# Talking-heads attention and two feed-forward layers on one core: the first chunk's loads, spreads and score copies in another order

## The chip, the core and the metric

One core of a Trainium2 chip runs the whole program. The metric is the device time of one execution in microseconds, the median of several runs; lower is better. TensorE (PE) multiplies, VectorE (DVE), ScalarE (ACT) and GpSimd (POOL) do elementwise work, each with a queue that is worked through in order. SyncE (SP) only issues DMAs; ScalarE can issue them too. The moves themselves are done by 16 DMA engines.

## The reference

```python
B, H, S, D = 2, 12, 448, 64          # q, k, v: (B, H, S, D), float32
scores = (q @ k^T) / sqrt(D)
scores = einsum('bhij,hg->bgij', scores, w_pre)     # mixes the 12 heads
attn   = softmax(scores, axis=-1)
attn   = einsum('bhij,hg->bgij', attn, w_post)      # mixes them again
x = (attn @ v) as (896, 768)
h = x @ w_in;  x = (h * clip(h + 3, 0, 6) / 6) @ w_out            # 768 -> 2048 -> 768
h = x @ w2_in; x = P(h) / (Q(h) + 1e-6) @ w2_out                  # P, Q: polynomials in h, |h|
```

Products are made to float32 precision from two parts: a high half (rounded) and a low half (the rest), and three matrix products of them.

## The kernel before

**Tiling.** A *chunk* is 120 query rows of one batch (88 in a batch's last one, nine groups), eight chunks in all; the code counts them from `C = 0`, the text calls them chunk one, two, three. A *group* is ten query rows of all 12 heads, 120 partitions; a chunk has 12 groups (`G`). `m` counts groups through all chunks.

**Scores.** `scores(C, hp)` makes two heads' scores of a chunk, 120 query rows by 448 keys each, into two PSUM banks `sc` (six products, line 267). Two copies (line 270) bring them to SBUF: one by ScalarE, one by VectorE.

**Spreads.** The mixing of heads wants the 12 heads of a query row in 12 partitions, so the scores are moved by DMA into `full`, 120 partitions by 12 groups by 448. For chunk one the copies go to one large tile `stage`, and `spread_group` moves one group at a time, 12 DMAs (line 252). From chunk two on, each head's copy `stg` is moved by `spread` as soon as it is made, 12 DMAs again (line 249), and a group can only be used when all 12 have landed. All are issued by SP.

**A step** of the loop over groups: `gsplit(m + 2)` makes the high half `sh` and low half `sl` of the group after next (lines 286 and 288, GpSimd; two buffers each), `premix(m)` mixes the heads (three products, lines 298 to 300, "mixing m"), takes the maximum (VectorE, line 302) and the exponential (ScalarE, line 304), `norm` and `weigh` put the sum's reciprocal into `wr`, `postmix(m - 2)` mixes again (line 333, "postmix"), and its result is copied to `at` (ScalarE, line 337) in the next step.

**Order.** It is written out by hand. In the loop over chunks, `SST` says in which steps the next chunk's score pairs are made, `QST` in which steps `q_prep` splits the q of the chunk after next (ScalarE the high half, VectorE the low), `AVST` in which the products with v are made (from chunk two on, for the chunk before). What a step makes is copied in the next one: the first pair's first half ahead of the split, its second half behind it, the second pair behind the maximum. Chunk one's scores and the first two pairs of chunk two come ahead of the loop. DMAs are issued in program order on SP; `load_q(C + 2)` and, in step 1 of chunk one, four `load_v` and `load_ab` (the small vectors pa, pb) are written in the loop but wait for nothing, and stand on SP ahead of the spreads, which wait for the copies. `build_ab` works on pa and pb in the first step of chunk two.

After the eight chunks the two feed-forward layers follow, from about 235 us on, in which TensorE works on 128x512 products.

Of the kernel before, what the change touches and what calls it, by code (L numbers as in the profile page):

```python
# [26 lines left out]
NP = H // 2  # L27
# [21 lines left out]
def fused_kernel(  # L49
# [201 lines left out]
    def spread_group(C, g, st):  # L251
        nc.sync.dma_start(out=full[C][:, g, :], in_=st.rearrange("(i g) h s -> g i (h s)", g=chunks[C][3])[g])

    def scores(C, hp, tags=("sc", "sc"), st=None, second=nc.vector.tensor_copy):
# [19 lines left out]
        post(2, lambda: take(0, nc.scalar.copy), lambda: take(1, second))  # L274
# [3 lines left out]
    def gsplit(m, eng=nc.gpsimd):  # L278
        if m >= len(groups):
            return  # L280
        C, g = groups[m]
        r = GP
        sh = att.tile([GP, S], F32R, tag="sh", bufs=2, name=f"sh{m}")
        sl = att.tile([GP, S], F32R, tag="sl", bufs=2, name=f"sl{m}")
        s = full[C][:, g, :]
        eng.tensor_scalar(out=sh[:r], in0=s[:r], scalar1=1.0, scalar2=0.0, op0=ALU.mult, op1=ALU.add)  # L286
        ssp[m] = (sh, sl)
        return eng.tensor_tensor(out=sl[:r], in0=s[:r], in1=sh[:r].bitcast(F32), op=ALU.subtract)  # L288
# [33 lines left out]
    def postmix(m):  # L322
# [9 lines left out]
        for jc in range(JC):  # L332
# [3 lines left out]
        aposts.append(  # L336
            lambda: nc.scalar.activation(out=at[C][:, :, :, c0 : c0 + rr], in_=av, func=AF.Copy)
        )
# [139 lines left out]
    for hp in range(NP):  # L478
# [3 lines left out]
        if hp == 1:  # L482
# [3 lines left out]
               nc.scalar.copy if hp == NP - 2 else nc.vector.tensor_copy)  # L486
        flush()
    for g in range(chunks[0][3]):
        spread_group(0, g, stage)
# [6 lines left out]
    first = gsplit(0, nc.vector)  # L496
    gsplit(1)
# [7 lines left out]
    flush()  # L505

# [41 lines left out]
    LAG = 2  # L548

# [10 lines left out]
    for C, (b, r0, n, G) in enumerate(chunks):  # L560
# [7 lines left out]
        sst = SST[G] if C else SST[G][: NP - FIRST]  # L568
        if nxt is not None:
            add([lambda h=h: scores(nxt, h) for h in range(0 if C else FIRST, NP)], sst)  # L570
        if C + 2 < len(chunks):
            add([lambda: q_prep(C + 2, 0, NP // 2), lambda: q_prep(C + 2, NP // 2, NP)], QST[G])
# [8 lines left out]
        for s in range(G):  # L581
            if s == 0 and C + 2 < len(chunks):
                load_q(C + 2)
            if C == 0 and s == 1:
                for i in range(4):
                    load_v(0, i)
                load_ab()
            if C == 1 and s == 0:
# [9 lines left out]
            for p in posts[:1]:  # L598
                p[1]()
            premix(m)  # L600
            if m >= 1 and not full_step:
# [360 lines left out]
```

## Time and profile before

| | |
|---|---|
| median of 3 runs | 714.84 us (712.84 to 715.27) |
| the profiled execution, its own time | 714.0 us |
| its span, first to last instruction | 712.3 us |
| TensorE busy | 695.3 us, 98% |
| VectorE busy | 555.4 us, 78% |
| ScalarE busy | 413.5 us, 58% |
| GpSimd busy | 261.1 us, 37% |
| mean granted clock of TensorE | 0.995 |

The times of the trace are microseconds from the first instruction of the profiled execution. A wait is read from the brackets at the end of a timeline row: how long the engine was idle before the row, and what ended it. Windows of the trace give the busy time of each engine, the granted clock of TensorE (1.00 is 2.4 GHz, 0.50 is 1.2 GHz), the mean busy share of the 16 DMA engines and the rate that they moved.

### The profile page before, as it was taken

To read this page: it belongs to the slowest core of one execution; us is meant where nothing else is said; L and a number is where in the kernel's file an instruction comes from. 1 tells how busy PE (TensorE), PEld (TensorE's weight loads), DVE (VectorE), ACT (ScalarE), POOL (GpSimd) and SP (SyncE) were. 2 spreads that over 40 slices of the span, in tenths; PEclk is the share of its full clock that TensorE was granted. 3 is DMA by queue.
4 is the path that set the end of the run, shared out by engine and by line. 5 is a ranking of instruction groups with operands and counts; after the bars stand their busy time and mean duration, and the time that the engine had idled before them with its cause. 6 is when DMAs were issued, how large, how long until landed. Compare 5 with 4: busy or idle time off the path is not lost.

```text
span 712.3 us, 12369 instructions
## 1 busy us (share of the span) xinstructions
PE 695.3 (98%) x4457; PEld 618.8 (87%) x4457; DVE 555.4 (78%) x925; ACT 413.5 (58%) x855; POOL 261.1 (37%) x259
## 2 busy tenths in 40 slices
PE   6999999999999999999999999999999999999997
PEld 3778888888889888889888888879999999889997
DVE  5565585665667689889997777888988899799991
ACT  5687887787887344334332221247666766579851
POOL 3887775877777333332444454400000000000000
PEclk9899999999999999999999999999999999999999
DMA  7625476555394544454354555364755766845522
GB/s 247 227 79 160 142 211 184 165 147 159 121 254 119 154 141 143 139 160 152 120 183 154 171 185 168 96 232 133 244 189 210 243 209 225 309 167 200 183 85 89
DMA packets 76033, 122.81 MB, mean 172 GB/s; under 512 B 6804, under 2 KB 56260, under 8 KB 75972
## 3 DMA queue, kind: packets, MB, share of 16 engines
q1 hardware_dynamic: 75684, 121.66, 53.8%
q8 instruction: 35, 0.57, 0.3%
q10 hardware_dynamic: 288, 0.37, 0.2%
q14 instruction: 26, 0.21, 0.1%
HBM read 83.39 MB, written 19.27 MB: 144 GB/s over the span
## 4 chain that ended last, share of the span: by engine, by line
PE 46%; DVE 31%; DMA 10%; ACT 6%; issue 5%; POOL 1%; SPq 0%; ACTq 0%; POOLq 0%; DVEq 0%
PE A L333 9%; DVE wf L425 7%; DVE wf L421 7%; PE X L353 5%; PE acc L379 4%; PE acc L378 4%; PE acc L377 4%; DMA pre<-wf 4%; PE sc L267 4%; DMA wraw<-in_moe_w_in_dram 4%; DVE gl L542 4%; DVE wf L419 4%; PE M L298 3%; PE h L378 3%; PE h L379 3%
## 5 line engine op out<-in xcount | busy, mean ns | idle before, releaser
L379 PE MATMUL h<-xh,wl 128*128 128x512 f32 (+1 forms) x384 | 141.0, 367 | 1.6 <-DVE wl L445 1.6
L377 PE MATMUL h<-xh,wh 128*128 128x512 f32 (+1 forms) x384 | 141.7, 369 | 0.0
L378 PE MATMUL h<-xl,wh 128*128 128x512 f32 (+1 forms) x384 | 140.7, 366 | 0.6 <-DVE xl L742 0.6
L417 ACT ACTIVATE wf<-wraw 128x768 f32<-128x768 f32 (+1 forms) x56 | 48.7, 877 | 98.4 <-DMA pre<-wf 55.9
L288 POOL TENSOR_TENSOR sl<-full,sh 120x448 fp32r<-120x448 f32 x89 | 102.4, 1150 | 7.4
L302 DVE TENSOR_REDUCE st<-M 120x1 f32<-120x448 f32 x90 | 56.1, 623 | 56.0 <-PE M L300 55.8
L333 PEld LDWEIGHTS A<-wr,e 120*112 120x112 f32 x720 | 86.5, 177 | 8.9 <-ACT wr L317 4.5
L333 PE MATMUL A<-wr,e 120*112 120x120 f32 x720 | 89.2, 267 | 2.0 <-ACT wr L317 1.9
L441 POOL TENSOR_SCALAR wh<-wf 128x768 fp32r<-128x768 f32 (+1 forms) x34 | 32.7, 962 | 138.5 <-DVE wf L425 135.8
L304 ACT ACTIVATE e<-M,st 120x448 f32<-120x448 f32 x90 | 57.2, 636 | 44.7 <-DVE st L302 44.6
L379 PEld LDWEIGHTS h<-xh,wl 128*128 128x128 f32 x384 | 72.1, 188 | 11.5 <-DVE wl L445 2.6
L378 PEld LDWEIGHTS h<-xl,wh 128*128 128x128 f32 x384 | 72.1, 188 | 8.9 <-DVE xl L742 0.9
L377 PEld LDWEIGHTS h<-xh,wh 128*128 128x128 f32 x384 | 72.1, 188 | 8.4 <-ACT wh L444 0.3
L286 POOL TENSOR_SCALAR sh<-full 120x448 fp32r<-120x448 f32 x89 | 55.3, 621 | 45.5 <-PE M L299 36.5
L379 PE MATMUL y<-gh,wl 128*128 128x384 f32 x192 | 70.2, 366 | 0.6 <-POOL wl L442 0.6
L377 PE MATMUL y<-gh,wh 128*128 128x384 f32 x192 | 70.4, 367 | 0.0
L378 PE MATMUL y<-gl,wh 128*128 128x384 f32 x192 | 70.2, 366 | 0.0
L442 POOL TENSOR_TENSOR wl<-wf,wh 128x768 fp32r<-128x768 f32 (+1 forms) x34 | 67.7, 1991 | 2.8
L421 DVE SCALAR_TENSOR_TENSOR wf<-wraw,icst,wf 128x768 int32<-128x768 int32 (+1 forms) x56 | 61.9, 1105 | 1.0
L419 DVE TENSOR_SCALAR wf<-wf 128x768 int32<-128x768 int32 x66 | 42.5, 643 | 24.0 <-ACT wf L417 23.8
L425 DVE SCALAR_TENSOR_TENSOR wf<-wraw,icst,wf 128x768 int32<-128x768 int32 (+1 forms) x56 | 57.7, 1032 | 0.6
L541 ACT ACTIVATE gh<-g 128x384 fp32r<-128x384 f32 (+1 forms) x32 | 18.6, 580 | 60.2 <-DVE g L539 59.9
(107 smaller groups left out, 1523.6 us busy)
## 6 DMA issues: line engine op xcount, KB each, us to landing
wraw<-in_moe_w_out_dram SPq DMA_DIRECT2D x28, 768.0 KB
wraw<-in_moe_w_in_dram SPq DMA_DIRECT2D x22, 768.0 KB
full<-stg SPq DMA_DIRECT2D x60, 210.0 KB
vraw<-in_v_dram SPq DMA_DIRECT2D x42, 224.0 KB
wpre<-in_moe_w_in_dram SPq DMA_DIRECT2D x10, 768.0 KB
w2h<-wh SPq DMA_DIRECT2D x16, 384.0 KB
w2l<-wl SPq DMA_DIRECT2D x16, 384.0 KB
wsh<-w2h SPq DMA_DIRECT2D x16, 384.0 KB
```

The costliest lines, as they stand in the source:

```text
L286: eng.tensor_scalar(out=sh[:r], in0=s[:r], scalar1=1.0, scalar2=0.0, op0=ALU.mult, op1=ALU.add)
L288: return eng.tensor_tensor(out=sl[:r], in0=s[:r], in1=sh[:r].bitcast(F32), op=ALU.subtract)
L302: nc.vector.tensor_reduce(out=st[:r, 0:1], in_=mt[:r, :S], op=ALU.max, axis=AX.X, negate=True)
L304: nc.scalar.activation(out=e[:r], in_=mt[:r, :S], func=AF.Exp, bias=st[:r, 0:1], accum_out=st[:r, 1:2])
L333: nc.tensor.matmul(av[:, jc], lhsT=e[:r, jc * JP : (jc + 1) * JP], rhs=wr[:r, :, :rr], start=True, stop=True)
L377: nc.tensor.matmul(o, lhsT=wh, rhs=mh, start=first, stop=False)
L378: nc.tensor.matmul(o, lhsT=wh, rhs=ml, start=False, stop=False)
L379: nc.tensor.matmul(o, lhsT=wl, rhs=mh, start=False, stop=last)
L419: nc.vector.tensor_scalar(out=wi, in0=wi, scalar1=3, scalar2=None, op0=ALU.logical_shift_left)
L421: nc.vector.scalar_tensor_tensor(out=wi, in0=hw, scalar=icst[:, 0:1], in1=wi, op0=ALU.bitwise_and, op1=ALU.bitwise_or)
L425: nc.vector.scalar_tensor_tensor(out=wi, in0=lw, scalar=icst[:, 1:2], in1=wi, op0=ALU.logical_shift_right, op1=ALU.bitwise_or)
L442: nc.gpsimd.tensor_tensor(out=lv, in0=w, in1=hv.bitcast(F32), op=ALU.subtract)
```

## The change

- `spread_group` takes the engine that issues it. Groups 1 and 3 of chunk one are spread by ScalarE, the ten others by SP.
- `load_q(2)` (q of chunk three) is issued behind the spreads of chunk one; the four `load_v` in step 9 of chunk one; `load_ab` in the first step of chunk two, `build_ab` in the first step of chunk three.
- The first two groups are split behind the last `q_prep` ahead of the loop: group 0 by VectorE as before, group 1 with its high half on ScalarE and its low half on VectorE instead of both on GpSimd.
- Chunk two's last four score pairs are made one at a time, in steps 1, 3, 5 and 7 instead of two each in steps 1 and 3. Both copies of a pair are made by VectorE, the second behind the maximum of the step. `q_prep` for chunk three moves from steps 8 and 9 to 6 and 8.
- The postmix results of groups 5, 7 and 9 are copied to `at` by VectorE.

```diff
-    def spread_group(C, g, st):
-        nc.sync.dma_start(out=full[C][:, g, :], in_=st.rearrange(...)[g])
+    def spread_group(C, g, st, eng):
+        return eng.dma_start(out=full[C][:, g, :], in_=st.rearrange(...)[g])
...
-        post(2, lambda: take(0, nc.scalar.copy), lambda: take(1, second))
+        post(2, lambda: take(0, first), lambda: take(1, second))
...
-        eng.tensor_scalar(out=sh[:r], in0=s[:r], scalar1=1.0, scalar2=0.0, op0=ALU.mult, op1=ALU.add)
+        if hi is not None:
+            hi.activation(out=sh, in_=s, func=AF.Copy)
+        else:
+            eng.tensor_scalar(out=sh[:r], in0=s[:r], scalar1=1.0, scalar2=0.0, op0=ALU.mult, op1=ALU.add)
...
+        if m in BYV:
+            aposts.append(lambda: nc.vector.tensor_copy(out=o, in_=av))
+        else:
+            aposts.append(lambda: nc.scalar.activation(out=o, in_=av, func=AF.Copy))
...
     for g in range(chunks[0][3]):
-        spread_group(0, g, stage)
+        last = spread_group(0, g, stage, nc.scalar if g in (1, 3) else nc.sync)
+    with tc.issue_after(last.ins):
+        load_q(2)
...
-    first = gsplit(0, nc.vector)
-    gsplit(1)
...
+    gsplit(0, nc.vector)
+    gsplit(1, nc.vector, nc.scalar)
...
+    ONES, BYV = [1, 3, 5, 7], (5, 7, 9)
...
-        sst = SST[G] if C else SST[G][: NP - FIRST]
+        sst = SST[G] if C else ONES
...
-            if s == 0 and C + 2 < len(chunks):
+            if s == 0 and C and C + 2 < len(chunks):
                 load_q(C + 2)
-            if C == 0 and s == 1:
+            if C == 0 and s == 9:
                 for i in range(4):
                     load_v(0, i)
+            if C == 1 and s == 0:
                 load_ab()
-            if C == 1 and s == 0:
+            if C == 2 and s == 0:
                 build_ab()
...
             gsplit(m + 2)
-            for p in posts[:1]:
-                p[1]()
+            if C:
+                for p in posts[:1]:
+                    p[1]()
             premix(m)
+            if not C:
+                for p in posts[:1]:
+                    p[1]()
```

The order of instructions at three places. First SP from q's load for chunk two on (`qraw_159` is chunk two's q, `qraw_307` or `qraw_261` chunk three's, `vraw` v; `full<-stage` are chunk one's spreads, `full<-stg` chunk two's). Before:

```order
L122 DMA qraw_159<-in_q_dram 128x720
L122 DMA qraw_307<-in_q_dram 128x720
L133 DMA vraw_0_321<-in_v_dram 112x512
L133 DMA vraw_1_323<-in_v_dram 112x512
L133 DMA vraw_2_325<-in_v_dram 112x512
L133 DMA vraw_3_327<-in_v_dram 112x512
L175 DMA pa<-in_moe_a_dram 128x4
L176 DMA pb<-in_moe_b_dram 128x2
L252 DMA full_176<-stage 120x1x448 x12
L249 DMA full_276<-stg_0_279 10x12x448 x2
L249 DMA full_276<-stg_1_292 10x12x448 x2
```

And now:

```order
L122 DMA qraw_159<-in_q_dram 128x720
L252 DMA full_176<-stage 120x1x448 x10
L122 DMA qraw_261<-in_q_dram 128x720
L249 DMA full_270<-stg_0_273 10x12x448 x2
L249 DMA full_270<-stg_1_286 10x12x448 x2
L249 DMA full_270<-stg_2_339 10x12x448 x2
L249 DMA full_270<-stg_3_396 10x12x448 x2
L249 DMA full_270<-stg_4_453 10x12x448 x2
L249 DMA full_270<-stg_5_511 10x12x448 x2
L133 DMA vraw_0_545<-in_v_dram 112x512
L133 DMA vraw_1_547<-in_v_dram 112x512
L133 DMA vraw_2_549<-in_v_dram 112x512
```

The loads of chunk three's q, of v and of pa and pb have left the place ahead of chunk one's spreads; the first stands between them and chunk two's, the others behind those.

ScalarE from its last high half of q ahead of the loop on (`e` is the exponential, `wr` the weights of the postmix). Before:

```order
L241 ACTIVATE qr<-qraw_159 128x480
L270 COPY stg_0_279<-sc_0_277 120x448
L270 COPY stg_1_292<-sc_2_290 120x448
L304 ACTIVATE e_319,st_317<-M_313,st_317 120x448
L304 ACTIVATE e_341,st_339<-M_335,st_339 120x448
L317 ACTIVATE wr_345<-wq,st_317 120x120
L317 ACTIVATE wr_367<-wq,st_339 120x120
L270 COPY stg_2_349<-sc_4_347 120x448
```

And now:

```order
L241 ACTIVATE qr<-qraw_159 128x480
L252 DMA full_176<-stage 120x1x448 x2
L271 COPY stg_0_273<-sc_0_271 120x448
L271 COPY stg_1_286<-sc_2_284 120x448
L288 ACTIVATE sh_303<-full_176 120x448
L308 ACTIVATE e_319,st_317<-M_313,st_317 120x448
L308 ACTIVATE e_331,st_329<-M_325,st_329 120x448
L321 ACTIVATE wr_335<-wq,st_317 120x120
```

Two DMA issues stand ahead of the two `stg` copies, a high half of group 1 behind them, and the copy of the next score pair is gone from here.

VectorE from the second maximum on, where the loop's first steps are. Before:

```order
L302 TENSOR_REDUCE st_339<-M_335 120x1
L312 TENSOR_SCALAR st_317<-st_317 120x1
L313 RECIPROCAL st_317<-st_317 120x1
L312 TENSOR_SCALAR st_339<-st_339 120x1
L313 RECIPROCAL st_339<-st_339 120x1
L270 COPY stg_2_349<-sc_5_348 120x448
L302 TENSOR_REDUCE st_381<-M_377 120x1
L270 COPY stg_3_358<-sc_7_357 120x448
L302 TENSOR_REDUCE st_404<-M_400 120x1
L312 TENSOR_SCALAR st_381<-st_381 120x1
L313 RECIPROCAL st_381<-st_381 120x1
L312 TENSOR_SCALAR st_404<-st_404 120x1
```

And now:

```order
L306 TENSOR_REDUCE st_329<-M_325 120x1
L316 TENSOR_SCALAR st_317<-st_317 120x1
L317 RECIPROCAL st_317<-st_317 120x1
L316 TENSOR_SCALAR st_329<-st_329 120x1
L317 RECIPROCAL st_329<-st_329 120x1
L271 COPY stg_2_339<-sc_4_337 120x448
L306 TENSOR_REDUCE st_360<-M_356 120x1
L271 COPY stg_2_339<-sc_5_338 120x448
L306 TENSOR_REDUCE st_381<-M_377 120x1
L316 TENSOR_SCALAR st_360<-st_360 120x1
L317 RECIPROCAL st_360<-st_360 120x1
L316 TENSOR_SCALAR st_381<-st_381 120x1
```

Where one copy of each of two pairs stood, both copies of one pair stand, on both sides of a maximum; the next pair follows two groups later.

## Rows read from the trace of the kernel before

**Rows 1.** The page's slices of the span, busy tenths, one engine a row.

```profile
PE   6999999999999999999999999999999999999997
```

**Rows 2.** The timeline's start: start, length in us, engine, line, operation, tiles, [idle].

```profile
0.79 2.80 SPq L157 DMA_DIRECT2D kraw<-in_k_dram  x6
...
3.81 0.58 ACT L233 ACTIVATE xh<-kraw 128x448 fp32r<-128x448 f32 x1 [0.83 <-DMA kraw<-in_k_dram]
...
16.37 0.39 DVE L286 TENSOR_SCALAR sh<-full 120x448 fp32r<-120x448 f32 x1 [2.51 <-DMA full<-stage]
...
16.91 0.52 PE L298 MATMUL M<-sh,wp_h 120*120 120x448 f32 x1 [4.08 <-DVE sh L286]
```

**Rows 3.** Stretches, all engines; the first row names the columns.

```profile
core 0: us, PE busy (x) PEld busy (x) DVE busy (x) ACT busy (x) POOL busy (x), PEclk, DMA share, GB/s
15.00:24.00 9.00, 6.96 (x24) 4.53 (x25) 3.47 (x10) 2.55 (x7) 5.52 (x7) 0.62 0.66 244
20.00:24.00 4.00, 4.00 (x18) 3.04 (x19) 1.76 (x7) 1.82 (x5) 3.01 (x4) 0.51 0.66 245
25.00:35.00 10.00, 9.40 (x69) 7.80 (x67) 5.62 (x19) 8.55 (x26) 8.40 (x11) 1.00 0.64 211
35.00:39.00 4.00, 3.57 (x26) 3.00 (x27) 2.22 (x8) 3.47 (x11) 3.72 (x5) 1.00 0.68 155
49.00:54.00 5.00, 5.00 (x40) 4.20 (x40) 3.30 (x11) 4.21 (x12) 3.85 (x6) 1.00 0.59 182
```

**Rows 4.** The timeline of SP: start, length of all issues of the row.

```profile
7.64 1.84 SPq L133 DMA_DIRECT2D vraw<-in_v_dram  x4
...
11.88 9.83 SPq L252 DMA_DIRECT2D full<-stage  x12
```

**Rows 5.** The timeline at the seam between chunk one and chunk two.

```profile
35.34 0.56 POOL L286 TENSOR_SCALAR sh<-full 120x448 fp32r<-120x448 f32 x1
...
37.10 0.56 POOL L286 TENSOR_SCALAR sh<-full 120x448 fp32r<-120x448 f32 x1
...
37.74 1.14 POOL L288 TENSOR_TENSOR sl<-full,sh 120x448 fp32r<-120x448 f32 x1
...
39.55 0.57 POOL L286 TENSOR_SCALAR sh<-full 120x448 fp32r<-120x448 f32 x1 [0.67 <-DMA full<-stg]
...
40.32 1.07 PE L333 MATMUL A<-wr,e 120*112 120x120 f32 x8
...
41.09 0.65 DVE L242 TENSOR_TENSOR ql<-qraw,qr 128x360 fp32r<-128x360 f32 x1
...
41.32 0.85 POOL L286 TENSOR_SCALAR sh<-full 120x448 fp32r<-120x448 f32 x1
...
41.66 0.53 DVE L180 TENSOR_SCALAR pa<-pa 128x4 f32<-128x4 f32 x1
...
42.25 1.14 POOL L288 TENSOR_TENSOR sl<-full,sh 120x448 fp32r<-120x448 f32 x1
...
44.81 0.47 PE L267 MATMUL sc<-xh,qr 64*120 64x448 f32 x2
```

**Rows 6.** DMA issues to 60 us: tiles, queue, count, size of one.

```profile
full<-stage SPq DMA_DIRECT2D x12, 210.0 KB
...
qraw<-in_q_dram SPq DMA_DIRECT2D x2, 360.0 KB
```

**Rows 7.** Three more stretches, the columns of rows 3.

```profile
4.00:7.00 3.00, 3.00 (x11) 1.32 (x11) 1.96 (x4) 2.33 (x6) 0.00 (x0) 1.00 1.05 369
...
9.00:10.00 1.00, 1.00 (x11) 0.53 (x8) 1.00 (x3) 1.00 (x4) 1.00 (x1) 1.00 0.93 301
...
120.00:121.00 1.00, 0.01 (x1) 0.00 (x0) 0.93 (x4) 1.00 (x4) 0.52 (x1) 1.00 0.77 232
```

**Rows 8.** The chain of waits, to 60 us: start, length, engine, tile, line.

```profile
19.90 2.52 PE sc L267 x12
...
44.88 1.41 PE sc L267 x12
```

More of the change, by code (lines that the diff above doesn't have):

```diff
@@ L249, in spread, with scores @@
         nc.sync.dma_start(out=to[:, : chunks[C][3]], in_=st[: chunks[C][3] * GR])
-    def spread_group(C, g, st):
-        nc.sync.dma_start(out=full[C][:, g, :], in_=st.rearrange("(i g) h s -> g i (h s)", g=chunks[C][3])[g])
-    def scores(C, hp, tags=("sc", "sc"), st=None, second=nc.vector.tensor_copy):
+    def spread_group(C, g, st, eng):
+        return eng.dma_start(out=full[C][:, g, :], in_=st.rearrange("(i g) h s -> g i (h s)", g=chunks[C][3])[g])
+    def scores(C, hp, tags=("sc", "sc"), st=None, first=nc.scalar.copy,
+               second=nc.vector.tensor_copy):
         n = chunks[C][3] * GR
@@ L272, in take, with gsplit @@
                 spread(C, 2 * hp + i, st[:, i])
-        post(2, lambda: take(0, nc.scalar.copy), lambda: take(1, second))
+        post(2, lambda: take(0, first), lambda: take(1, second))
     ssp = {}
-    def gsplit(m, eng=nc.gpsimd):
+    def gsplit(m, eng=nc.gpsimd, hi=None):
         if m >= len(groups):
@@ L335, in postmix @@
             )
-        aposts.append(
-            lambda: nc.scalar.activation(out=at[C][:, :, :, c0 : c0 + rr], in_=av, func=AF.Copy)
-        )
+        o = at[C][:, :, :, c0 : c0 + rr]
+        if m in BYV:
+            aposts.append(lambda: nc.vector.tensor_copy(out=o, in_=av))
+        else:
+            aposts.append(lambda: nc.scalar.activation(out=o, in_=av, func=AF.Copy))
     xps = {}
@@ L485, in fused_kernel @@
         scores(0, hp, (("M", "A"), ("sc", "sc"))[hp % 2], stage[:, 2 * hp : 2 * hp + 2],
-               nc.scalar.copy if hp == NP - 2 else nc.vector.tensor_copy)
+               second=nc.scalar.copy if hp == NP - 2 else nc.vector.tensor_copy)
         flush()
     for g in range(chunks[0][3]):
-        spread_group(0, g, stage)
+        last = spread_group(0, g, stage, nc.scalar if g in (1, 3) else nc.sync)
+    with tc.issue_after(last.ins):
+        load_q(2)
     build_mix()
@@ L566, in add @@
                 sched.setdefault(steps[i * len(steps) // len(units)], []).append(u)
-        sst = SST[G] if C else SST[G][: NP - FIRST]
+        sst = SST[G] if C else ONES
         if nxt is not None:
-            add([lambda h=h: scores(nxt, h) for h in range(0 if C else FIRST, NP)], sst)
+            kw = {} if C else {"first": nc.vector.tensor_copy}
+            add([lambda h=h: scores(nxt, h, **kw) for h in range(0 if C else FIRST, NP)], sst)
         if C + 2 < len(chunks):
-            add([lambda: q_prep(C + 2, 0, NP // 2), lambda: q_prep(C + 2, NP // 2, NP)], QST[G])
+            add([lambda: q_prep(C + 2, 0, NP // 2), lambda: q_prep(C + 2, NP // 2, NP)], QST[G] if C else [6, 8])
         if C == NCH - 2:
```

## The prediction

> **What bounds the kernel now.** I read the page's slices first. TensorE is full from the third slice to the last [rows 1], so in most of the program only a shift of the whole row of work can save time. What can still be moved is the first 45 us: TensorE stands still for 4.08 us before the first mixing product at 16.91 [rows 2], and then runs at half clock from about 17 to 24 us [rows 3]. From 49 to 54 us it is busy all of the time [rows 3]. So the question is by how much the change moves 44.81, the first scores of chunk three; all that follows is released by earlier work of the program and shifts with it.
>
> The next view is DMA by stretches [rows 3]. From 15 to 24 us the 16 DMA engines are 0.66 busy at 244 GB/s, from 25 to 35 us 0.64 at 211, while SP has spreads queued all along. A share that doesn't move, with a queue behind it, reads as 10 of the 16 engines fully busy and six idle (10/16 = 0.63). The 120 partitions of a spread are ten rows of twelve heads, which fits ten. The trace has a second sign. SP issues a spread every 9.83/12 = 0.82 us [rows 4], but 210 KB (215,000 bytes [rows 6]) at 244 GB/s take 0.88 us. So the spreads wait for the DMA engines and not for SP. In the Trainium skill, "DMA: Bandwidth & Descriptors", section "Why a DMA increments its semaphore by 16 and not by 1" says that a copy from ScalarE or SyncE uses the largest number up to 16 that divides the slowest dimension on both sides, the lowest-numbered engines of the 16; for 120 and 10 that is 10, and the flat 0.64 to 0.66 agrees.
>
> The third view is the queue of GpSimd at the seam between chunk one and chunk two [rows 5]. It works through a group every 1.76 us (35.34, 37.10), is done with the last of chunk one at 38.88, then is idle for 0.67 us until 39.55, and what it waits for is the spreads of chunk two (`full<-stg`). All 12 of these must have landed before the first split of chunk two. Behind 39.55 there is a chain with one order: split 12, split 13 (low half done at 43.39), the last product of mixing 13, postmix 11, the scores at 44.81. That is 5.26 us.
>
> **The sum, part by part.** The change has two ends. The head of chunk one starts earlier; the tail, chunk two's spreads, is what 44.81 hangs on. I cost the tail.
>
> *Loads behind the spreads.* Before, v's four loads are in the DMA engines when spread 0 is issued at 11.88, and it is used at 16.37, 4.49 us later [rows 2, 4]. Into empty engines the first load of k, issued at 0.79, is used at 3.81, 3.02 us later [rows 2]. Spread 0 will be nearer to that, since q's load for chunk two is then the only one ahead: I take 3.3 us, 15.2 us, so 1.2 us earlier; the bounds are 1.5 and 0. All later spreads go at the engines' own pace, so the whole queue shifts by 1.2.
>
> *But q's load for chunk three now stands between the spreads of chunk one and those of chunk two.* It is 360 KB [rows 6]. At 369 GB/s (4 to 7 us, all 16 engines) it takes 1.0 us, at 301 (9 to 10 us) 1.2 [rows 7]. Before, it ran ahead of everything, at a time when the ten engines had nothing more urgent to do. Term: +1.0, bounds 0.9 and 1.3. v's loads and the pair pa and pb come behind chunk two's spreads and cost the queue nothing.
>
> *The spreads of chunk two themselves.* There are as many as before, 12. From 25 to 35 us they run at 211 GB/s: 1.02 us each [rows 3]. Copied singly in steps 2, 4, 6 and 8 instead of in pairs in 2 and 4, the last of them is ready at about 32.7 us (mixing 0 at 16.1, eight steps of 1.85, two copies and a maximum) instead of about 30. With 3.3 us from issue to landing it could be used at 36.0, plus half a microsecond for the end of the wait, 36.5. The engines get to it later than that (sum below), so the later copies cost nothing; that cover is gone if the engines get through 2.6 us earlier. At the end q's load for chunk four no longer runs beside the last spreads (35 to 39 us: 155 GB/s at a share of 0.68 [rows 3]); v's loads do, in larger pieces. I take -0.2, bounds -1.0 and +0.3.
>
> *Two spreads on ScalarE.* SP's ten issues end 1.6 us sooner, but the DMA engines had the longer pace already (0.88 against 0.82). Term: 0, bounds -0.2 and 0. On ScalarE the two issues (about 0.8 us each, as on SP) push its two `stg` copies from 12.06 to about 13.7; SP wants these only at 20.6, so they cost nothing. The same skill page, section "Issuing engines are not separate DMA queues", says that copies started from different engines run on the same 16 DMA engines and that only the time of issuing is saved. By that rule the term is 0 as well; no row of this trace shows two queues at work on spreads.
>
> *First groups.* Split 1 goes from GpSimd (0.57 + 1.15) to ScalarE and VectorE (about 0.6 + 0.62), which brings mixing 1 forward, and GpSimd begins with group 2 when its spread has landed: 15.2 + 2 x 0.88 = 17.0, or 17.8 if ScalarE's spreads go between. It then needs 10 x 1.76 = 17.6 us and is ready for group 12 at 35.4; before, it was at 38.88. All of this, and whatever is saved of the half-clock stretch, ends in a longer wait for chunk two's spreads. Value: 0, covered by that wait.
>
> *Work moved from ScalarE to VectorE.* Four score copies (0.62 each) and three postmix copies go to VectorE, which is busy 5.62 of 10 us from 25 to 35, where ScalarE is busy 8.55 [rows 3]. Both are covered by the same wait.
>
> *VectorE at the seam.* Beside split 13, whose high half takes 0.85 us instead of 0.57, VectorE has q's low half (41.09) and `build_ab` (41.66) [rows 5]. The change puts the one a step or more ahead and the other one chunk later, where GpSimd has slack. Split 13 is on the chain: -0.3, bounds -0.3 and 0.
>
> Sum at 44.81: -1.2 + 1.0 - 0.2 + 0 - 0.3 = **-0.7 us**. The wait for chunk two's spreads then ends at 39.55 - 0.4, about 39.15, while GpSimd has stood ready since 35.4. In the profiled execution that is a span of 712.3 - 0.7 = 711.6 us and 713.3 of its own 714.0. The three runs have a median of 714.84 (712.84 to 715.27), 0.84 above the profiled one; from there **714.1 us**. The smallest difference from no change that a measurement of this kernel can tell is about 0.3%, 2.1 us, so this counts as the same.
>
> **Rivals.** *The queue empties in time (faster).* If chunk two's spreads ran at chunk one's pace, 0.88 instead of 1.02, twelve would save 1.7 us: 714.1 - 1.7 = 712.4. The floor is the 36.5 above, where the last copy decides: 2.65 us better than 39.15, 711.4. For it: the fall from 244 to 211 GB/s may come from neighbours that the change moves. Against it: chunk three's spreads, which don't fill the engines, give 182 GB/s at a share of 0.59, 308 for a full share, against 370 in chunk one (244/0.66) and 330 in chunk two (211/0.64) [rows 3]; the second kind of spread looks slower everywhere.
>
> *A second stretch at half clock (slower).* With the first chunk ready early, TensorE has nothing to do between the end of postmix 9 (35.4 + 2.5, the distance from 38.88 to 41.39, where postmix 9 ends [rows 5], 37.9) and mixing 12 (39.8), and little until 41. Before 16.91 it stood for 4.08 us and the clock fell at about 17.1 (a mean of 0.62 over the 9 us up to 24 is 6.8 us at half clock [rows 3]); a gap of 1 us near 120 us left it at 1.00 [rows 7]. Mine is some 2 us, between the two. If the clock fell it would fall on the stretch in which TensorE is the bound. Price: four heads' scores take 2.52 us at half clock and 1.41 at full [rows 8]; 6.8 us at that pace do about 4 us of work, 2.8 are lost. 714.1 + 2.8 = 716.9. It decides from the point where the wait at the seam is long enough; the better the head of chunk one gets, the likelier it is.
>
> *ScalarE's two spreads find idle DMA engines (faster).* Six engines are idle. Were they taken, two spreads, 1.8 us, would leave the queue: 712.3. The page named above excludes it.
>
> *The change doesn't do what it says.* The order shows the loads behind the spreads, and ScalarE's two right behind its last part of q, so only their price could differ.
>
> **How the numbers follow.** The forecast 714.1 has 0.55 (its own range 713.0 to 715.2), the queue that empties 0.28 (711.4 to 712.7), the second half clock 0.10 (716.0 to 717.5), ScalarE's own engines 0.03, and 0.04 is left for others. Of these, faster by over 0.3% is 0.26 + 0.03 + 0.01 = 0.30; slower is 0.07 + 0.03 = 0.10, since a part of that rival ends within the bound; the rest, 0.60, is within 0.3%. The range from 711.2 to 716.6 leaves out the edge of the first rival and the upper of the second, with a little for the scatter of the runs.
>
> **What would show it.** Right: the first split at about 15.2 to 15.8; share of DMA flat at 0.66 from 14 us on with a bulge near 25 where q's load runs; GpSimd idle for 3 to 4 us ahead of chunk two's first split, waiting for `full<-stg`, and that split at about 39.15; scores of chunk three at about 44.1. The first rival: that split before 37.8. The second: a granted clock under 1.00 between 38 and 50 us. The sum is wrong if spread 0 lands no earlier than 16, if the stretch from 26 to 38 moves far from 211 GB/s, or if the work behind 45 us doesn't shift with it.

## The result, and the profile after

The changed kernel has a median of 717.4 us (713.13 to 718.82, 11 runs) against 713.3 of the kernel before in the same comparison: a ratio of 1.0054, 95% interval 1.0038 to 1.0071. It is slower, by 3.9 us, where 714.1 and "the same" were forecast, and 717.4 lies above the range. The forecast was reckoned from 714.84, a median of three runs; as a difference it was -0.7 us. The profiled execution took 718.82 with a span of 717.1: it is the longest of the eleven, and its waits are likely to be long ones.

TensorE's slices and its granted clock on the page:

```profile
PE   7969999999999999999999999999999999999998
...
PEclk9979999999999999999999999999999999999999
```

The third slice, about 36 to 54 us, holds a new hole and a lower clock, where [rows 1] was full. The head of chunk one did what it should. The timeline's start (columns as in rows 2), and then SP's issues:

```profile
11.76 2.54 ACTq L252 DMA_DIRECT2D full<-stage  x2
...
14.62 0.39 DVE L290 TENSOR_SCALAR sh<-full 120x448 fp32r<-120x448 f32 x1 [0.71 <-DMA full<-stage]
...
15.16 0.43 PE L302 MATMUL M<-sh,wp_h 120*120 120x448 f32 x1 [2.47 <-DVE sh L290]
```

```profile
11.76 10.30 SPq L252 DMA_DIRECT2D full<-stage  x10
22.10 0.86 SPq L122 DMA_DIRECT2D qraw<-in_q_dram  x1
23.07 10.62 SPq L249 DMA_DIRECT2D full<-stg  x12
33.74 3.44 SPq L133 DMA_DIRECT2D vraw<-in_v_dram  x4
38.16 0.65 SPq L122 DMA_DIRECT2D qraw<-in_q_dram  x1
```

The first split comes at 14.62 instead of 16.37 [rows 2], and TensorE waits for it 2.47 us instead of 4.08. But chunk two's spreads are all issued only at 33.69, and v's four loads and q's for chunk four stand right behind them. The last spread can't be issued sooner: its copy ends at 32.90 (32.29 and 0.61), where 32.7 was forecast, and it is issued at 32.94; before, the last one was issued at 32.54.

```profile
32.29 0.61 DVE L271 COPY stg<-sc 120x448 f32<-120x448 f32 x1
```

```profile
32.94 0.76 SPq L249 DMA_DIRECT2D full<-stg  x1
```

The seam, where [rows 5] had 0.67 us of idle GpSimd:

```profile
34.29 1.14 POOL L292 TENSOR_TENSOR sl<-full,sh 120x448 fp32r<-120x448 f32 x1
...
36.94 0.98 PE L337 MATMUL A<-wr,e 120*112 120x120 f32 x8
...
43.22 0.56 POOL L290 TENSOR_SCALAR sh<-full 120x448 fp32r<-120x448 f32 x1 [7.79 <-DMA vraw<-in_v_dram]
43.84 0.73 PE L302 MATMUL M<-sh,wp_h 120*120 120x448 f32 x1 [5.92 <-POOL sh L290]
...
45.59 1.80 PE L337 MATMUL A<-wr,e 120*112 120x120 f32 x8
...
50.04 0.69 PE L268 MATMUL sc<-xh,qr 64*120 64x448 f32 x2
...
51.68 0.46 PE L302 MATMUL M<-sh,wp_h 120*120 120x448 f32 x1
```

GpSimd is through with chunk one at 35.43 and then waits 7.79 us. Split 12 reads only `full`; the row names v's load as the last to come, which says that v's loads and the last spreads were in the DMA engines together. TensorE stands still for 5.92 us, and a postmix then takes 1.80 us instead of 0.98. The stretches (columns of rows 3) show why:

```profile
15.00:24.00 9.00, 8.84 (x45) 6.25 (x46) 6.33 (x18) 5.93 (x16) 6.84 (x9) 0.81 0.68 209
...
28.00:34.00 6.00, 6.00 (x47) 5.32 (x46) 5.56 (x13) 4.07 (x11) 5.45 (x7) 1.00 0.66 236
...
35.00:39.00 4.00, 2.50 (x19) 2.24 (x19) 2.76 (x9) 3.18 (x10) 0.43 (x1) 1.00 1.01 228
39.00:42.00 3.00, 0.00 (x0) 0.00 (x0) 0.00 (x0) 0.00 (x0) 0.00 (x0) 0.72 0.93 195
42.00:45.00 3.00, 1.10 (x2) 0.47 (x2) 0.00 (x0) 0.00 (x0) 1.69 (x3) 0.50 0.65 137
45.00:49.00 4.00, 3.94 (x16) 3.69 (x17) 1.30 (x4) 1.52 (x4) 3.83 (x6) 0.50 0.06 11
```

Two things are to be seen. From 35 to 39 all 16 DMA engines are busy, and yet they move 228 GB/s, no more than the 236 that they moved from 28 to 34, with spreads alone, at a share of 0.66. So the six engines that v's loads bring in add nothing in this stretch; that what they carry is taken from the spreads is concluded from this total and from the late split. And from the stretch that begins at 39 the granted clock is below 1.00, at 0.50 from 42 to 49, the lower of its two levels (1.2 GHz).

From split 12 to mixing 14 it takes 8.46 us (43.22 to 51.68) where it took 6.67 before (39.55 to 46.22). Mixing 14 in the kernel before:

```profile
46.22 0.46 PE L298 MATMUL M<-sh,wp_h 120*120 120x448 f32 x1
```

The split is 3.67 later and this way 1.79 longer, together 5.46; 4.8 of it are in the span (717.1 against 712.3).

### The profile page after: what moved, and what is told of

It is laid out like the page before. It is cut to its first block, busy times and chain, and to the rows that moved or that the text cites. A ratio compares the mean times of both kernels' runs of the same rounds, so it can differ in the third digit from the quotient of the medians.

```text
span 717.1 us, 12369 instructions
## 1 busy us (share of the span) xinstructions
PE 696.2 (97%) x4457; PEld 620.6 (87%) x4457; DVE 560.1 (78%) x933; ACT 411.5 (57%) x849; POOL 258.3 (36%) x257
## 4 chain that ended last, share of the span: by engine, by line
PE 46%; DVE 31%; DMA 11%; ACT 6%; issue 5%; POOL 1%; SPq 0%; ACTq 0%; POOLq 0%; DVEq 0%
PE A L337 9%; DVE wf L427 7%; DVE wf L431 7%; PE X L359 5%; PE acc L385 4%; PE acc L383 4%; PE acc L384 4%; DMA pre<-wf 4%; PE sc L268 4%; DVE gl L550 4%; DVE wf L425 4%; PE M L302 3%; PE h L384 3%; PE h L383 3%; PE h L385 3%
## 5 line engine op out<-in xcount | busy, mean ns | idle before, releaser
L337 PEld LDWEIGHTS A<-wr,e 120*112 120x112 f32 x720 | 88.5, 179 | 7.1 <-ACT wr L321 2.5
```

The costliest lines, as they stand in the source:

```text
L337: nc.tensor.matmul(av[:, jc], lhsT=e[:r, jc * JP : (jc + 1) * JP], rhs=wr[:r, :, :rr], start=True, stop=True)
```

## The experiments

Each ratio is to the kernel before on the same chip, with its 95% interval. "Split 12" is chunk two's first split, "way" the time from it to mixing 14, "idle" TensorE's idle time right ahead of mixing 12, all in the profiled execution, and "half" says if the granted clock fell between 38 and 50 us there. A profile is one execution and the DMA engines' pace differs between executions, so time is judged by the ratios, and the profiles are read for what goes with what. The mean granted clock of an execution counts every fall in it, the one at the head of chunk one too: it was 0.995 in e1's profile, where the clock fell at the seam, and 0.994 in e14's, where it did not.

| kernel | q for chunk three | v's loads | rest as | ratio | split 12 | idle | way | half |
|---|---|---|---|---|---|---|---|---|
| before | ahead | ahead | before | 1 | 39.55 | - | 6.67 | no |
| after | between | behind | after | 1.0054 (1.0038, 1.0071) | 43.22 | 5.92 | 8.46 | yes |
| e7 | ahead | ahead | after | 0.9999 (0.9980, 1.0017) | 39.59 | 0.22 | 6.47 | no |
| e1 | between | ahead | after | 1.0017 (0.9996, 1.0038) | 42.09 | 4.22 | 7.39 | yes |
| e5 | ahead | behind | after | 1.0016 (0.9994, 1.0037) | 38.80 | 1.01 | 7.53 | yes |
| e4 | ahead | behind | before | 1.0006 (0.9994, 1.0019) | 40.98 | 2.43 | 8.64 | yes |
| e9 | between | ahead | before | 1.0025 (1.0005, 1.0045) | 38.88 | - | 6.67 | no |
| e6 | between | behind | before | 1.0032 (1.0015, 1.0049) | 41.11 | - | 6.66 | no (but from 32) |
| e12 | between | ScalarE, later | after | 1.0032 (1.0010, 1.0054) | 38.87 | 1.78 | 8.75 | yes |
| e11 | ahead | ScalarE, later | after | 0.9986 (0.9970, 1.0003) | 37.85 | 0.91 | 6.49 | no |
| e8 | ahead | ScalarE, later | before | 0.9986 (0.9965, 1.0007) | 37.74 | - | 6.66 | no |

**First theory and its rivals.** T: v's loads run beside chunk two's last spreads and slow them. S: the single score pairs and copies make the spreads late. Q: q's load in between does. C: the clock alone.

*e1, v's loads ahead again.*

```diff
-            if C == 0 and s == 9:
+            if C == 0 and s == 1:
                 for i in range(4):
                     load_v(0, i)
```

> The changed kernel with one part undone: v's four loads stand at step 1 of chunk one again, ahead of chunk one's spreads on SyncE's queue; everything else is as changed. Theory T (v's loads, issued at 33.7 right behind chunk two's spreads, run beside the last four or so of them and slow them, so that chunk two's first split waits until 43.2, TensorE stands idle for 5.9 us and falls to half clock): the first split of chunk two comes at 38 to 39.5, no stretch at half clock after 38, scores of chunk three at 43.5 to 45, and 712.5 to 714.5, within 0.3% of before. Rival S (the score pairs taken singly and the copies on VectorE make the last spreads late): the split stays at 42 or later and the time at 716.5 to 718. Rival Q (q's load for chunk three in between is the cost): the split comes at 42 or later, since that load stays where it is.

Median 714.91, ratio 1.0017. More than half of the loss goes (1.0054 to 1.0017), so v's place counts. Its profile, one of the longest of its twelve executions, still has split 12 at 42.09, with spreads alone named as what it waited for, so T is not all of it:

```profile
42.09 0.57 POOL L290 TENSOR_SCALAR sh<-full 120x448 fp32r<-120x448 f32 x1 [6.09 <-DMA full<-stg]
```

*e2, v's and chunk four's loads behind chunk three's first spreads.* The edit moves `load_v(0, i)` and `load_q(3)` to step 3 of chunk two.

> The changed kernel with v's four loads, and with them q's load for chunk four, moved further back: to step 3 of chunk two, on SyncE's queue behind chunk three's first four spreads; only the small loads pa and pb still stand right behind chunk two's spreads. Theory T: nothing large runs beside chunk two's last spreads, so its first split comes at 37 to 38.5, TensorE is idle for under 2 us there, no half clock after 38, 711 to 713. By rival S or Q: the split at 42 or later, 716.5 to 718. If the later place of v's loads costs something itself, it shows as a wait for v at the values' products of chunk one (after 55) or as chunk three's spreads landing late.

Median 717.56, ratio 1.0061 (1.0042 to 1.0080). The profiled execution came near what T says (split 12 at 38.97 where 37 to 38.5 was expected, 712.35), but it is the shortest of six, and four of the others took 717 or more. A miss by time; what those waited for isn't seen. e12 asks the same in a cleaner way.

*e4, v's loads alone.* The kernel before with `load_v` in step 9.

> The kernel before with one thing moved: v's four loads go from step 1 to step 9 of chunk one, on SyncE's queue behind chunk two's spreads and ahead of q's load for chunk four; score pairs, copies and spreads as before, q's load for chunk three ahead of the first spreads as before. Theory T: chunk one's first split 0.5 to 1.2 earlier than 16.4, chunk two's first split at 41.5 to 43.5 instead of 39.55, TensorE idle for 4 to 6 us ahead of it, 714.5 to 717. Rival S: without the single score pairs nothing is late, the split at 38.5 to 39.5 and 712 to 713.5.

Median 712.95, ratio 1.0006. The profile shows T's mechanism (split 12 at 40.98, waiting for v, half clock), but that is the longest of its twelve executions. Moving v's loads alone, with what it gains at the head and what it costs at the seam, changes nothing in the median: T in its simple form falls, and S seems to have a point.

**Second theory** (Q+V, and later A, in the expectations): the two loads add up. Its rivals are that v's loads cost only together with the rest of the change (V+rest), the rest alone (R), and q's load only where v's are behind (B). The next four take q, v and the rest apart.

*e5, q's load ahead again (v's behind).* `load_q(C + 2)` in the first step for C = 0 too, no `issue_after`.

> The changed kernel with q's load for chunk three put back ahead of chunk one's spreads; v's four loads stay behind chunk two's. By the runs so far, v's loads put there alone (score pairs, copies and spreads as before) left the time at 712.95, and taken away from there brought the changed kernel from 717.4 to 714.9. Theory Q+V (the queue of chunk two's spreads has room for one of the two loads, not for both: q's load in between makes the last spreads start and land about a microsecond later, and so more of them run beside v's): chunk two's first split at 40 to 41.5 instead of 43.2, 713 to 714.5. Theory V+rest (v's loads cost only together with the single score pairs and the copies on VectorE): split at 42.5 or later, 716.5 to 718.

*e6, both loads moved and nothing else.*

> The kernel before with the two loads moved as in the change, and nothing else: q's load for chunk three behind chunk one's spreads, v's four loads behind chunk two's. Score pairs, copies, splits and spreads as before. Theory Q+V: this is the whole loss, the split at 42 to 43.5, TensorE idle for 4 to 6 us ahead of it, 715.5 to 718. Theory V+rest: 712.5 to 714, since the single pairs and the copies are not there.

*e7, everything but the two loads.*

> The changed kernel with both loads, q's for chunk three and v's, put back ahead of chunk one's spreads: what is left of the change are the two spreads by ScalarE, the single score pairs, the copies on VectorE, the splits' order and the late small loads pa and pb. Theory Q+V: neutral, chunk one's first split at 16 to 17, chunk two's at 39 to 40, 712.5 to 714. Theory V+rest: neutral too, 712.5 to 714. Theory R (the rest alone is late: the last spreads are issued later): split at 41 or later, 715 to 717.

*e9, q's load alone.*

> The kernel before with only q's load for chunk three moved behind chunk one's spreads; v's loads stay ahead of them. By the ratios so far q's load in between is worth +1.9 us where v's loads are late and the rest is undone (1.0032 against 1.0006), +1.3 where v's are early and the rest is as changed (1.0017 against 0.9999). Theory A (the two loads add up on the ten engines that the spreads use): chunk one's first split 0.2 to 0.6 earlier than 16.4, chunk two's at 40.5 to 41.5 instead of 39.55, 714.2 to 715.2, a ratio of 1.002 to 1.003. Theory B (q's load costs only where v's run behind the spreads): a ratio under 1.001.

Medians 713.8, 715.39, 712.24 and 714.35; ratios in the table. The times came as Q+V and A say, or within 0.3 us of it, but the splits of three profiles did not: 38.80 in e5 (40 to 41.5 expected), 41.11 in e6 (42 to 43.5), 38.88 in e9 (40.5 to 41.5). e7 speaks against S: ScalarE's two spreads, the single pairs, the copies on VectorE and the order of the splits together are worth nothing (0.9999, within 0.002); added to moved loads they give 0.0010 (e4 to e5), 0.0022 (e6 to after) and -0.0008 (e9 to e1). Between rows that differ in one thing only, q's load in between costs 0.0038 (e5 to after), 0.0018 (e7 to e1), 0.0026 (e4 to e6) and 0.0025 (e9), on the mean 0.0027 or 1.9 us; v's loads behind cost 0.0037 (e1 to after), 0.0017 (e7 to e5), 0.0007 (e9 to e6) and 0.0006 (e4), on the mean 0.0017 or 1.2 us. Each of these has an error of about 0.002, so that the two add up is shown only roughly. In e1, e4, e5 and e9 neither alone makes 0.0054; e2, which has q's load in between and no v beside chunk two's spreads, does (1.0061), and that isn't explained.

Nor is the price of q's load always paid at split 12. Over the five pairs that differ in its place, split 12 moves by -0.67 us (before to e9), 0.13 (e4 to e6), 1.02 (e11 to e12), 2.50 (e7 to e1) and 4.42 (e5 to after). In the order of the kernel before there is a second way. `stg` shares five buffers with k's raw loads, and in e6 the copies of chunk two's last pair wait until an earlier spread has given one back; the next `wr` comes late, TensorE is idle for 1.98 us, and its clock falls there (columns of rows 3 in the second view):

```profile
29.20 0.62 DVE L270 COPY stg<-sc 120x448 f32<-120x448 f32 x1 [1.94 <-DMA full<-stg]
...
31.45 1.07 PE L333 MATMUL A<-wr,e 120*112 120x120 f32 x8 [1.98 <-ACT wr L317]
```

```profile
32.00:36.00 4.00, 4.00 (x20) 3.70 (x19) 0.85 (x3) 2.76 (x8) 1.74 (x3) 0.57 0.69 218
```

The same copy on VectorE waits 0.72 us in e9 and 1.76 in e10, and not in the profiles of the kernel before, of e4 and of the changed kernel. It waits 0.97 in e8 too, where chunk one's groups come early, so it isn't q's load alone that brings this wait.

*e10, one more load in between.* The kernel before with 224 KB of v loaded into a spare buffer behind chunk one's spreads.

> The kernel before with one more load put in between: 224 KB of v, in 112 packets of 2048 bytes, behind chunk one's spreads on SyncE's queue, into a buffer that nothing reads; all other loads stay where they are. It asks what of q's load (270 KB in 768 packets of 360 bytes) makes its price. If bytes do: 0.8 of what q's load costs there, a ratio of 1.0015 to 1.0025. If the count of packets does: under a fifth of it, a ratio of 1.000 to 1.0006. If any load does, by taking turns with the spreads' packets: as much as q's or more.

Median 714.55, ratio 1.0025 (1.0007 to 1.0043). The expectation takes the size of the wrong q: chunk three's load, which stands in between, has 360 KB [rows 6]; the 270 KB are chunk four's. So what is shown is only that a load of fewer bytes in larger pieces costs there as well: 0.62 of the bytes, and the same ratio as e9, with an error that allows half as much.

*e8 and e11, no load in between or behind.* Both leave q's load for chunk three ahead and let ScalarE issue the other five in steps 1 to 5 of chunk two, e8 on the kernel before, e11 on the changed one. e12 is the same on the changed kernel with q's load in between.

```diff
+            if C == 1 and 1 <= s <= 4:
+                load_v(0, s - 1, nc.scalar)
+            if C == 1 and s == 5:
+                load_q(3, nc.scalar)
```

> The kernel before with v's four loads and q's load for chunk four taken out of SyncE's queue and issued by ScalarE, one a step, in steps 1 to 5 of chunk two, that is after chunk two's first split: nothing stands ahead of chunk one's spreads but q's load for chunk three, and nothing runs beside chunk two's last spreads. Both theories: chunk one's first split at 15 to 15.8, chunk two's at 37.5 to 38.8, no wait for v at the values' products, 711.3 to 712.6, faster than both kernels. If ScalarE's five issues (some 0.5 each) hold up the weights of the mixing steps, 713 to 714; if the time stays at 713, the first split of chunk two does not set the end.

> The changed kernel with q's load for chunk three ahead of the first spreads again, and v's four loads and q's for chunk four issued by ScalarE in steps 1 to 5 of chunk two, after its first split: the score pairs, copies and spreads of the change with no load in between or behind. By theory A chunk two's first split comes at 36.5 to 38, 710.5 to 712, ahead of both kernels and of the kernel before with the same loads moved (711.6). If the faster groups of chunk one (GpSimd done with them at 35.4 instead of 38.9) only make TensorE wait longer at the seam, the time is that of the other, 711 to 712.5, or worse by 1.5 where the clock falls.

> The changed kernel with v's four loads and q's for chunk four issued by ScalarE in steps 1 to 5 of chunk two; q's load for chunk three stays in between, as changed. Nothing but the small loads pa and pb runs beside chunk two's last spreads. Theory A: 1.0 to 1.9 us over the same kernel with q's load early, so 712 to 714, a ratio of 0.999 to 1.002. If q's load in between is enough for the loss, as the variant with v's loads on SyncE's queue at step 3 gave (717.6), 716 to 718; then the later place of v's loads was not to blame there.

Medians 711.61, 712.52 and 715.38. e8 came as expected; e11 is no faster than e8 and just above its range, and e12 is a miss: slower than theory A said, and less slow than its rival. e11 and e12 are the best pair of the study: the same instructions but for the place of one load. DMA share from 30 to 46 us in 40 slices of 0.4 us, in tenths, of the changed kernel, e11 and e12:

```profile
DMA  6676666666679799999989969999875666775110
```

```profile
DMA  6567566656657532110000000001004780186100
```

```profile
DMA  6666666666667665421000000000010003881000
```

Without loads behind the spreads the engines are empty by about 38; in the changed kernel they are full from about 35 to 42. e12 is later than e11 by q's load. The timeline of e11 and then of e12:

```profile
36.58 0.98 PE L337 MATMUL A<-wr,e 120*112 120x120 f32 x8
...
38.48 0.46 PE L302 MATMUL M<-sh,wp_h 120*120 120x448 f32 x1 [0.91 <-POOL sh L290]
...
40.00 0.98 PE L337 MATMUL A<-wr,e 120*112 120x120 f32 x8
...
44.34 0.46 PE L302 MATMUL M<-sh,wp_h 120*120 120x448 f32 x1
```

```profile
36.73 0.98 PE L337 MATMUL A<-wr,e 120*112 120x120 f32 x8
...
39.49 0.46 PE L302 MATMUL M<-sh,wp_h 120*120 120x448 f32 x1 [1.78 <-POOL sh L290]
...
41.24 1.80 PE L337 MATMUL A<-wr,e 120*112 120x120 f32 x8
...
47.62 0.47 PE L302 MATMUL M<-sh,wp_h 120*120 120x448 f32 x1
```

Mixing 12 starts 1.01 later in e12, which is q's load. But mixing 14 starts 3.28 later: TensorE was idle for 1.78 us instead of 0.91, its clock fell, and each postmix takes 1.80 instead of 0.98. In these two executions the wait costs 1.0 and the clock that falls after it 2.3. The sum agrees with the ratios, which are 0.0046 apart, or 3.3 us. The spans of the two are 6.8 us apart; what is more than 3.3 arises later, most of it after 485 us, in the feed-forward layers, which are the same in both. e12's is one of the longest of its twelve executions, e11's one of the shortest.

**Third theory**, K: most of the loss is the clock; its rival W: the wait alone. Products of 128x512 in bf16, whose result nothing uses, fill the idle stretch:

```diff
+            if m == 12:
+                for i in range(N):
+                    nc.tensor.matmul(pd, lhsT=warm[:, :128], rhs=warm, ...)
```

*e3, the changed kernel with 24 of them.*

> The changed kernel with 24 products of 128x512 in bf16 put ahead of chunk two's first mixing, on TensorE alone (their result is not used): they fill the wait and leave everything else as it is. It tells the price of the clock from the price of the wait. Theory T: the split still comes at 43 to 43.5, but the granted clock stays at 1.00 from 38 to 50; the way from that split to the scores of chunk three is 5.3 us as before instead of 6.8, so the time falls by 1.5 to 2.5 to 715 to 716, and 1.7 to 2.7 over before are left for the wait alone. Rival C (the clock alone makes the loss): 713 to 714. Rival N (the clock costs nothing by the end): 717 to 718.

*e13, the changed kernel with 12.*

> The changed kernel with 12 products of 128x512 in bf16 (0.21 each, 2.6 in all; their result is not used) ahead of chunk two's first mixing, half as many as before, so that they end at about 40.5, ahead of the split at 43.2, and hold up nothing. Theory K (most of the loss is the clock that falls after the idle stretch): if they hold the clock, 715 to 716, a ratio of 1.003 to 1.004; the 2.7 left idle behind them may still let it fall, then 717 to 718 as changed. Theory W (the wait alone makes the loss): 717 to 718 even where the mean clock is 0.995 or more.

Neither helped: medians 717.69 and 717.85, ratios 1.0064 (1.0048 to 1.0080) and 1.0053 (1.0033 to 1.0073). In e3 the mean clock was high (0.995 or more in all six executions), but at the seam of its profile it fell all the same, after 1.61 us left idle behind the products, which last until 42.75, and the way is 7.54:

```profile
44.36 0.46 PE L302 MATMUL M<-sh,wp_h 120*120 120x448 f32 x1 [1.61 <-POOL sh L290]
```

```profile
47.00:50.00 3.00, 3.00 (x16) 2.70 (x16) 0.87 (x4) 2.00 (x7) 2.83 (x5) 0.57 0.00 0
```

In executions in which the split comes sooner than here (43.74) the products can hold up mixing 12 themselves. So e3 can't part clock from wait. In e13 3.88 us stayed idle behind the products and the clock fell as before (0.50 in the profile from 44 to 50). So 12 products were too few for the wait of the changed kernel, and 24 did not hold the clock in the profile either.

*e14, e12 with 8 of them.*

> The variant with v's loads by ScalarE and q's load for chunk three in between (1.0032) with 8 of those products (1.7 in all) in the idle stretch of 1.78 ahead of chunk two's first mixing. Theory K: no half clock after 38 in nearly all runs, the way from mixing 12 to mixing 14 takes 5.9 instead of 8.1, a ratio of 1.000 to 1.0015, 712.8 to 714. Theory W: the ratio stays at 1.002 to 1.0045, 714.5 to 716.

Median 712.27 against 715.38 without, ratio 0.9984 (0.9964 to 1.0004) against 1.0032 (1.0010 to 1.0054): by time K is upheld, and the gain is larger than it said. From 41 to 44 us e12 and then e14 (columns of rows 3):

```profile
41.00:44.00 3.00, 3.00 (x13) 2.75 (x13) 0.85 (x3) 1.52 (x4) 2.83 (x4) 0.50 0.19 34
```

```profile
41.00:44.00 3.00, 2.68 (x19) 2.16 (x18) 1.45 (x5) 1.38 (x4) 2.92 (x4) 1.00 0.04 10
```

That the products made this difference is not shown by these two executions. In e14's, TensorE was later anyway, since its head ran longer at half clock (0.62 from 15 to 24 us, 0.81 in e12): mixing 11 begins at 37.90 instead of 36.03, so that hardly a wait was left, and the products held up mixing 12:

```profile
37.90 0.45 PE L302 MATMUL M<-sh,wp_h 120*120 120x448 f32 x1
...
39.41 1.89 PE L613 MATMUL dummy<-warm 128*128 128x512 bf16 x8
40.96 0.55 PE L302 MATMUL M<-sh,wp_h 120*120 120x448 f32 x1
```

K rests on the times of the executions. Of twelve executions of e12 seven have a mean granted clock of 0.993 or less, and these take 713.9 to 719.0; of e14 one has. With q's load in between, v's loads out of the way and these products, the changed order is no slower than the kernel before.

*e15, e11 with 6 of them.*

> The variant with all loads out of the way (q's for chunk three ahead of the first spreads, v's and q's for chunk four by ScalarE in steps 1 to 5 of chunk two, score pairs, copies and spreads as changed; 0.9986) with 6 of those products (1.3) ahead of chunk two's first mixing. Theory K: the runs of it in which the clock fell (0.993, 713.8 to 714.8) go, 710.8 to 712.2, a ratio of 0.9965 to 0.9985, faster than before. Theory W: 712 to 713, as without them.

Median 711.05 (709.75 to 711.89), ratio 0.9961 (0.9947 to 0.9975): 0.4% faster than the kernel before, and so faster than both. All six executions have a mean clock of 0.995 or more. What the six products add to e11 is not shown: the intervals of the two ratios overlap, and e11's own profile has no fall of the clock at the seam. Its timeline at the seam, where no idle time is left ahead of mixing 12:

```profile
38.11 1.46 PE L611 MATMUL dummy<-warm 128*128 128x512 bf16 x6
39.35 0.46 PE L302 MATMUL M<-sh,wp_h 120*120 120x448 f32 x1
...
45.21 0.46 PE L302 MATMUL M<-sh,wp_h 120*120 120x448 f32 x1
```

*e16, e5 with 8 of them.*

> The changed kernel with q's load for chunk three ahead of the first spreads (v's four loads stay behind chunk two's spreads; 1.0016) and with 8 of the products (1.7 in all) ahead of chunk two's first mixing. Theory K (the later split costs about what it is late, and the clock that falls after it as much again): mean clock 0.995 or more in most runs, a ratio of 0.997 to 1.0005, 711.5 to 713.8. Theory W (the wait alone): 1.001 to 1.003, as without the products.

Median 712.33, ratio 1.0010 (0.9989 to 1.0031): between the two theories, and it settles nothing by time. Its profile is the one that shows products holding the clock: without them TensorE would have been idle from about 39 to 42.37, yet the clock stays at 1.00 and the way takes 6.47, so there v's loads cost a wait and no more (columns of rows 3 in the second view):

```profile
38.92 1.89 PE L610 MATMUL dummy<-warm 128*128 128x512 bf16 x8
42.37 0.46 PE L302 MATMUL M<-sh,wp_h 120*120 120x448 f32 x1 [1.56 <-POOL sh L290]
```

```profile
44.00:47.00 3.00, 2.94 (x22) 2.15 (x22) 1.70 (x6) 1.98 (x5) 2.83 (x4) 1.00 0.03 7
```

## Why the prediction was wrong, point by point

**What bounds the kernel: right as to place, wrong as to the resource.** In the changed kernel the end hangs on chunk two's first split, and what follows shifts with it. (In e8 and e9, in the order of the kernel before, GpSimd waits ahead of this split for TensorE, 1.11 and 1.72 us, and not for the spreads.) But "10 of the 16 engines fully busy" made the six others look free. They are not free capacity: 16 busy engines moved 228 GB/s, two thirds of them 236. In the Trainium skill, "DMA: Bandwidth & Descriptors", section "Queues, rings and completion order" says that on each DMA engine work is taken in the order of its ring; by that v's loads can run ahead only on the engines that the spreads don't use, and the rise from 0.66 to 1.01 agrees. What the page's rule doesn't give, and the total and the late split point to, is that the spreads pay for it.

**Loads behind the spreads, -1.2: about right where nothing large stands behind, lost where it does.** The first split came 1.75 earlier, beyond the bound of 1.5. Where v's loads leave the head and don't run beside chunk two's spreads either (nor q's for chunk four), the time gains 0.0014 (before to e8) and 0.0013 (e7 to e11), about 1 us, each with an error of 0.002. e4, which has the gain at the head and v's loads behind, stands at 1.0006. In the changed kernel, though its head is 1.75 earlier, the last spread is issued 0.4 later than before (32.94 against 32.54), right behind its copy, since the single pairs are copied in later steps.

**q's load in between, +1.0: too small in time, and not settled at the split.** e11 to e12 gives 1.02 at the split, but that this is the forecast is luck: the five pairs of profiles give -0.67 to 4.42. In time it costs 1.9 us on the mean of four pairs and 3.3 in e11 to e12 (0.0046). In e11 to e12 the clock makes the difference.

**The tail, -0.2 with bounds -1.0 and +0.3: the term that failed.** It rested on "v's loads come behind chunk two's spreads and cost the queue nothing". Between e12 and the changed kernel only v's loads and chunk four's q differ, and split 12 comes at 38.87 against 43.22: +4.35 in these two profiles. e11 to e5 and e8 to e4 differ in the same way and give +0.95 and +3.24. In time the three pairs give 0.0022, 0.0030 and 0.0020, or 1.4 to 2.1 us and 1.7 on the mean, where the forecast had nothing. By bytes it is no surprise: 4 x 224 + 270 KB are 1.19 MB, at 228 GB/s 5.2 us of what all engines together move there. I had costed a load by its place in the queue instead of by its bytes. This term isn't the whole miss, which is 4.6 us (3.9 against -0.7). The averages above, -1.0 for the head, +1.9 for q's load and +1.7 for v's, make 2.6; some 1.3 are left, about as much as these averages are uncertain. In these prices the fall of the clock is contained, which the forecast had put into a rival.

**ScalarE's spreads, first groups, copies, VectorE at the seam: about right.** ScalarE's two issues took 2.54 us instead of 1.6, ahead of copies that SP wanted only at 23.07. GpSimd was ready for group 12 at 35.43 (35.4 was forecast), and e7 puts all of it at 0.9999. The -0.3 of VectorE at the seam isn't told apart in that.

**The rival of the second half clock: the mechanism was right and its price near, its chance was not.** It stood at 716.9 with 0.10. That 717.4 lies so near is in part luck, since it had the split at 39.15 and the profile has it at 43.22. The way from split 12 to mixing 14 takes 6.47 to 6.49 in the changed order at full clock (e7, e11) and 8.46 to 8.75 with a long stretch at half (after, e12): 2.0 to 2.3 against the forecast 2.8. I expected some 2 us of idle time in the forecast itself and knew only that 4.08 had let the clock fall and 1 us had not. e12 fell after 1.78, so the forecast itself may well have met it. The forecast and this rival should have been weighed as one case, since the longer the wait, the likelier both.

What stays open: how the 3.9 us of the median part into wait and clock in the changed kernel itself (in the profile 3.67 and about 2.0, less what the end of the program takes back), how often the clock falls at the seam in executions without a profile, and why e2 was slow.

## What to carry to other kernels

Cost a transfer by the bytes that it takes from whatever runs beside it, not by its place in the queue: behind the last urgent transfer is beside it. Where a change lengthens a wait ahead of TensorE, price the clock that falls after the wait together with the wait; from e11 to e12 a microsecond more of wait cost three. Eight products that nobody needs cost less than they gained in e14; where much of the wait stayed idle beside them, in e13, they gained nothing. And ask which buffers a transfer gives back: where it is late, the copies that want them stand still too.

## What the runs showed of the hardware that was not expected

- DMA engines that were idle beside copies from SBUF to SBUF gave little or no more throughput when loads ran on them: 236 GB/s at a share of 0.66, 228 at 1.01 (the changed kernel, 28 to 34 and 35 to 39 us). From 36 to 38 us, with loads beside the spreads, it was 264 at 1.04 in e16 and 221 at 1.05 in the changed kernel. Ahead of the spreads loads alone moved 369 [rows 7].
- Idle stretches of about the same length ended differently: the clock fell after 1.01 us without a product (e5), after 1.61 behind filling products (e3) and after 1.78 (e12), and did not after 0.91 (e11) and after 1.56 behind filling products (e16). Where it fell, the way to mixing 14 was 0.9 to 2.3 us longer than the 6.47 of the changed order. In the Trainium skill, "TensorE: Matmul & The Clock Gate", section "HAM oscillation — how this bites in real kernels" tells of the same chain, a wait for DMA and then a clock that has fallen, and the rows of e12 agree.
